# Attention, a gated block and four experts on one core: sums of h's tiles by accumulating transfers, signs in the gating, rest units on 64x64 quarters, and another list of work

## The chip, the core and the metric

One program on 1 core of a Trainium2 chip. The metric is the device time of the whole program in microseconds. TensorE (PE; PEld is its weight load), VectorE (DVE), ScalarE (ACT), GpSimd (POOL) and SyncE (SP, which issues the transfers) each run an instruction list of their own and wait for each other by semaphores.

## The reference

Three parts stand one behind the other, all in float32 (4 batches of 576 tokens, 8 heads of 64):

```python
kv = einsum('bhsd,bhse->bhde', k, v)
out = einsum('bhsd,bhde->bhse', q, kv)
x = out / sqrt(mean(out * out, -1) + 1e-6) * g_norm      # -> (2304, 512)

a, b = x @ w1, x @ w2                                     # 512 -> 1024
x = ((a * b) @ w3) @ w_out                                # -> (2304, 512)

p = probs / (probs.sum(-1) + 1e-9)                        # 4 experts
y = sum(p[:, e] * (maximum(x @ ew1[e], 0) @ ew2[e]) for e in range(4))
```

## The kernel before

Every large product is made of three TensorE passes on fp32r halves: high times high, low times high, high times low (lines 349, 350 and 351, function `mm3`). An operand is split into a high and a low tile by `split` (a cast, line 394, and a subtraction, line 399). Tiles are 128 partitions by 512 elements, 256 KB.

The work of the front part is written as a list of names, `FRONT`, and each name is a function that adds operations with an engine, a cost and the tiles it reads and writes. A planner (`Plan.order`) walks them in time: an engine takes the ready operation that stands earliest in the list, within a window, if tiles and PSUM banks are free. The result is a fixed order per engine; SP and GpSimd are engines of this plan like the others. The experts' part follows in a loop over three groups of tokens.

The parts that matter here:

- `unit b p` is attention for a batch and a pair of heads: loads of q, k and v, the product of keys and values (`outer_by_head`, line 803, 64x64 instructions, two heads in turn; `outer`, line 819), transposes of q (line 770), the product with q (line 847), and the norm (`normed_turned`; its root runs on GpSimd, lines 684 and 685). The last 64 tokens of each batch don't fill a tile; `rest_unit g` takes those of two batches for all heads. It writes the transposed q into two zeroed tiles `qr`, one for each batch, and line 883 makes 8 products of 128x128, two adding up in a place. An fp32 instruction of TensorE shows as two records.
- `bilinear_pair` and `bilinear_plain` make h = a * b from x, w1 and w2, by a scheme of seven products of sums in place of eight (Strassen's, in Winograd's form), and keep some tiles of h in DRAM (`ab0kept`, `ab1kept`).
- `row` and `turn` make w3 @ w_out once, `w3o`, with the sums of its blocks in `w3o_summed`.
- `mixed_product g n` multiplies h by w3o, seven products for each of two pairs of batches (`PAIR_PRODUCTS`): a11 b11, a12 b21, s2 t2, s1 t1, s3 t3, s4 b22, a22 -t4. Here t1 = b12 - b11, t2 = b22 - t1, t3 = b22 - b12 and -t4 = b21 - t2 are sums of h's tiles: 32 subtractions on VectorE (line 1240), each then split. Each product is four steps of six full-width products; its result is copied out of PSUM (`copied`) or added (`plus`, line 1274).
- After the front, expert weights are loaded (`e1raw`, `e2raw`, line 371), split, combined and stored to DRAM (`we`, `w2kept`; lines 384 and 1539), and loaded again for each group (line 1797 for w).

## Time and profile before

| | before |
|---|---|
| time, median of 3 runs | 1094.87 us (1094.67 to 1096.27) |
| the profiled execution | 1096.5 us |
| its span | 1094.7 us |
| TensorE busy | 1085.6 us, 99% |
| VectorE busy | 862.2 us, 79% |
| ScalarE busy | 634.2 us, 58% |
| GpSimd busy | 47.7 us, 4%, 61 instructions |
| moved by DMA | 286.5 MB, mean 262 GB/s |

The page is read by stage, since its shares are means over stages with different limits. Attention and the products for h lie between 0 and about 246 us, w3 @ w_out until 284, the products of h with it until 372, and the experts behind. A matmul's length in a timeline overlaps the next one's; the pace is the distance between starts.

### The profile page before, as it was taken

To read this page: it belongs to the slowest core of one execution; us is meant where nothing else is said; L and a number is where in the kernel's file an instruction comes from. 1 tells how busy PE (TensorE), PEld (TensorE's weight loads), DVE (VectorE), ACT (ScalarE), POOL (GpSimd) and SP (SyncE) were. 2 spreads that over 40 slices of the span, in tenths; PEclk is the share of its full clock that TensorE was granted. 3 is DMA by queue.
4 is the path that set the end of the run, shared out by engine and by line. 5 is a ranking of instruction groups with operands and counts; after the bars stand their busy time and mean duration, and the time that the engine had idled before them with its cause. 6 is when DMAs were issued, how large, how long until landed. Compare 5 with 4: busy or idle time off the path is not lost.

```text
span 1094.7 us, 18502 instructions
## 1 busy us (share of the span) xinstructions
PE 1085.6 (99%) x6411; PEld 987.4 (90%) x6411; DVE 862.2 (79%) x1692; ACT 634.2 (58%) x1369; POOL 47.7 (4%) x61
## 2 busy tenths in 40 slices
PE   8999999999999999999999999999999999999998
PEld 7888888888888999999899999999999999999998
DVE  4888989889988887888788874567688866485896
ACT  6888647888765655844564565534455555443531
POOL 6513000000000000000000000000000000000000
PEclk9999999999999999999999999999999999999999
DMA  9989798864500799989999997777779867676756
GB/s 325 307 265 334 273 345 271 250 160 89 174 1 7 263 356 349 333 302 295 364 350 328 342 347 250 273 250 256 251 262 353 296 232 246 233 278 223 274 163 196
DMA packets 177538, 286.50 MB, mean 262 GB/s; under 512 B 36388, under 2 KB 85028, under 8 KB 177444
## 3 DMA queue, kind: packets, MB, share of 16 engines
q1 hardware_dynamic: 177120, 285.05, 77.8%
q8 instruction: 51, 0.84, 0.3%
q14 instruction: 43, 0.35, 0.1%
q10 hardware_dynamic: 324, 0.26, 0.1%
HBM read 198.22 MB, written 82.84 MB: 257 GB/s over the span
## 4 chain that ended last, share of the span: by engine, by line
PE 93%; DMA 4%; DVE 1%; SPq 1%; ACT 1%; issue 0%; ACTq 0%; DVEq 0%
PE b L350 24%; PE b L349 24%; PE b L351 24%; PE b L1821 19%; PE b L770 1%; PE b L847 1%; DMA e1raw<-in_moe_w_dram 1%; DMA kv<-in_v_dram 1%; DMA w<-w2kept 1%; DMA w1raw<-in_moe_w_dram 1%; DMA kv<-in_k_dram 1%; PE b L803 1%; PE b L819 0%; SPq L371 0%; DMA e2raw<-in_moe_w_dram 0%
## 5 line engine op out<-in xcount | busy, mean ns | idle before, releaser
L1821 PE MATMUL b<-w,hth 128*128 128x512 f32 x588 | 208.4, 394 | 0.1
L758 ACT COPY u<-b 128x384 f32<-128x384 f32 (+1 forms) x183 | 91.9, 502 | 196.2 <-PE b L351 194.5
L1657 DVE TENSOR_TENSOR u<-u,b 128x384 f32<-128x384 f32 x144 | 79.4, 552 | 110.0 <-PE b L351 52.0
L1821 PE MATMUL b<-w,htl 128*128 128x256 f32 x588 | 156.0, 279 | 0.0
L1821 PEld LDWEIGHTS b<-w,hth 128*128 128x128 f32 x588 | 108.9, 188 | 19.6 <-DVE acc L1849 0.5
L1821 PEld LDWEIGHTS b<-w,htl 128*128 128x128 f32 x588 | 110.7, 188 | 3.0
L1849 DVE SCALAR_TENSOR_TENSOR acc<-b,pn,acc 128x512 f32<-128x512 f32 x123 | 85.5, 745 | 29.8 <-PE b L1821 29.5
L394 ACT CAST hth<-s 128x384 fp32r<-128x384 f32 x144 | 69.7, 512 | 44.0 <-DVE s L1757 43.3
L1668 ACT ACTIVATE u<-u 128x384 f32<-128x384 f32 x108 | 56.9, 527 | 47.0 <-DVE u L1657 46.8
L399 DVE TENSOR_TENSOR htl<-s,hth 128x384 fp32r<-128x384 f32 x144 | 75.5, 550 | 6.2 <-ACT hth L394 6.1
L399 DVE TENSOR_TENSOR htl<-u,hth 128x384 fp32r<-128x384 f32 x108 | 55.9, 550 | 2.2 <-ACT hth L394 2.2
L351 PE MATMUL b<-wdh,htl 128*128 128x512 f32 x144 | 56.7, 393 | 0.0
L350 PE MATMUL b<-wdl,hth 128*128 128x512 f32 x144 | 56.6, 393 | 0.0
L349 PE MATMUL b<-wdh,hth 128*128 128x512 f32 x144 | 56.0, 389 | 0.0
L394 ACT CAST hth<-u 128x384 fp32r<-128x384 f32 x107 | 51.2, 510 | 0.3
L349 PE MATMUL b<-w,hth 128*128 128x256 f32 x168 | 47.6, 283 | 0.7 <-DMA w<-w2kept 0.7
L350 PE MATMUL b<-w,hth 128*128 128x256 f32 x168 | 47.5, 283 | 0.0
L351 PE MATMUL b<-w,htl 128*128 128x256 f32 x168 | 47.5, 283 | 0.0
L349 PE MATMUL b<-th,weh 128*128 128x512 f32 x112 | 44.1, 394 | 0.0
L350 PE MATMUL b<-tl,weh 128*128 128x512 f32 x112 | 43.7, 390 | 0.0
L351 PE MATMUL b<-th,wel 128*128 128x512 f32 x112 | 43.6, 389 | 0.0
L1757 DVE TENSOR_TENSOR s<-u 128x384 f32<-128x384 f32 x72 | 37.5, 550 | 3.4 <-ACT u L1668 3.4
(310 smaller groups left out, 3150.8 us busy)
## 6 DMA issues: line engine op xcount, KB each, us to landing
w<-w2kept SPq DMA_DIRECT2D x126, 512.0 KB, 4.9
we<-we SPq DMA_DIRECT2D x240, 256.0 KB, 5.0
we<-weh SPq DMA_DIRECT2D x48, 256.0 KB, 3.5
we<-wel SPq DMA_DIRECT2D x48, 256.0 KB, 3.6
e2raw<-in_moe_w_dram SPq DMA_DIRECT2D x20, 512.0 KB, 5.5
w3raw<-in_moe_w_dram SPq DMA_DIRECT2D x16, 512.0 KB, 4.6
e1raw<-in_moe_w_dram SPq DMA_DIRECT2D x16, 512.0 KB, 4.8
w2kept<-wth SPq DMA_DIRECT2D x32, 256.0 KB, 3.9
```

Of the source, the lines that this page charges most:

```text
L349: nc.tensor.matmul(ps, w[0], x[0], start=first, stop=False, skip_group_check=more)
L350: nc.tensor.matmul(ps, w[0], x[1], start=False, stop=False, skip_group_check=more)
L351: nc.tensor.matmul(ps, w[1], x[0], start=False, stop=last, skip_group_check=more)
L394: nc.scalar.copy(to(dst.high.tile), value(src.tile))
L399: nc.vector.tensor_tensor(out=to(dst.low.tile), in0=value(src.tile), in1=to(dst.high.tile), op=ALU.subtract)
L758: lambda e: nc.scalar.copy(to(dst.tile), value(src.tile)) if e == "act"
L770: nc.tensor.transpose(ps[:, c], raw[:, c], ident)
L1657: lambda _: nc.vector.tensor_tensor(out=t[:, :W], in0=base[:, :W], in1=ps[:, :W], op=ALU.add),
L1668: lambda eng: nc.scalar.activation(out=t[:, :W], in_=src[:, :W], func=ACTF.Relu)
L1757: lambda eng: nc.vector.tensor_tensor(out=t[:, :W], in0=x[:, :W], in1=y[:, :W], op=op),
L1821: nc.tensor.matmul(ps.tile if whole_width else ps[:, 0:256], (h.high if whole_width else h.low)[:, c], both if whole_width else raw[:, r, ...
L1849: nc.vector.scalar_tensor_tensor(out=a.tile, in0=ps.tile, scalar=sc, in1=a.tile, op0=ALU.mult, op1=ALU.add)
```

## The change

- The 32 subtractions for t1 to t4 go from VectorE to the DMA: SP copies a tile (`copy_of`), and GpSimd issues a transfer that adds another tile to it (`added`, with `accum_op=ALU.add`). For t1, b12 is added to in place where it lies in the core's memory. That is 32 accumulating transfers and 16 more copies of 256 KB.
- A transfer can add and not subtract, so some of h's tiles get a minus sign: `negative` says which, and `times_signed` puts it into the multiplication that makes the tile. The seven products, their order and the signs of their results follow: `s1 t1` comes first, and results leave PSUM negated (`turned_round`) or by subtraction (`less`).
- The sums of blocks of weights are made in their own tile: two operations of 256 columns and one of 512 in place of four of 256 (`block_weights`, `w3o_summed`).
- A rest unit copies the transposed q once, whole (`qt`), and makes 16 products of 64x64, each on one of four quarters of TensorE, in place of 8 of 128x128; `qr` and its zeroing go; its norm reads two banks.
- `FRONT` is another list, in which units, rest units, weights and rows of w3 stand in other places.

TensorE's instructions are otherwise the same in number and form. The diff, cut to its core (of `FRONT` the first line):

```diff
-THREE_BANKS = ((0, 3), (1, 3))
+THREE_BANKS = ()
-EARLY = (0, 1, 2, 3, 4, 5, 6, 7, 8, 9, 12, 16)
+EARLY = (0, 1, 2, 3, 4, 5, 6, 7, 8, 9, 10, 12, 16)
+REST_INNER = 0.68
...
-    "norm_scale, weight 1 4, unit 0 0, unit 1 0, unit 1 1, weight 1 0, unit 1 3, unit 1 2, unit 0 1, unit "
+    "norm_scale, weight 1 4, unit 0 0, unit 1 0, unit 1 3, weight 1 0, unit 1 1, unit 1 2, unit 0 1, unit "
...
-        qs = []
-        while len(rest_q) < 2:
-            rest_q.append(zeroed("qr"))
-        for i in range(2):
-            s = rest_q[i]
-
-            def cut(t, c=slice(i * REM, (i + 1) * REM)):
-                return t.rearrange("p (h c) -> p h c", h=HP)[:, :, c]
-
-            evacuate(s, pq, 256, cut, cut)
-            qs.append(s)
-        po = bank()
+        qt = half("qt")
+        evacuate(qt, pq, 512, whole, whole)
+        po = [bank(), bank()]
 
         def inner(e):
-            for h in range(HP):
-                c = slice(h * P, (h + 1) * P)
-                for i in range(2):
-                    own, at = kvb[2 * g + i][h // 2], h % 2 * 2 * P
+            for p in range(HP):
+                for h, i in ((0, 0), (1, 1), (1, 0), (0, 1)):
+                    rows = slice(h * D, (h + 1) * D)
+                    own, at = kvb[2 * g + i][p // 2], p % 2 * 2 * P + h * (P + D)
                     nc.tensor.matmul(
-                        po[:, c], qs[i][:, c],
-                        own[:, at:at + 2 * P].rearrange("p (b c) -> p b c", c=D)[:, 0:4:3], start=i == 0, stop=i == 1,
+                        po[h][i * REM:(i + 1) * REM, p * D:(p + 1) * D],
+                        qt[rows, p * P + i * REM:p * P + (i + 1) * REM], own[rows, at:at + D],
+                        start=True, stop=True,
                     )
 
-        add({"pe": 1.72}, inner, reads=qs + kvb[2 * g] + kvb[2 * g + 1], writes=[po])
+        add({"pe": REST_INNER}, inner, reads=[qt] + kvb[2 * g] + kvb[2 * g + 1], writes=po)
...
+    def times_signed(t, x, sign):
+        if sign > 0:
+            nc.vector.tensor_tensor(out=t, in0=t, in1=x, op=ALU.mult)
+        else:
+            nc.vector.scalar_tensor_tensor(out=t, in0=x, scalar=sign, in1=t, op0=ALU.mult, op1=ALU.mult)
+
+    def negative(b, f):
+
+        return b < B and (b % 2 == 1) == (f < KF // 2)
...
-            lambda e: nc.vector.tensor_tensor(out=t[:, :n], in0=t[:, :n], in1=pb[:, :n], op=ALU.mult),
+            lambda e: times_signed(t[:, :n], pb[:, :n], sign),
...
+            s21 = half("s21")
+            left, right = (bufs[0], 0), (bufs[1], 1)
+
+            def sums(n, make, reads, writes):
+                add({"dve": t_dve(n)}, lambda _: nc.vector.tensor_tensor(**make()), reads=reads, writes=writes)
+
+            sums(256, lambda: dict(out=block(0, 0), in0=block(0, 1), in1=block(0, 0), op=ALU.subtract), [], [left])
+            sums(
+                512, lambda: dict(
+                    out=blocks(s21.tile), in0=block(1, 1).unsqueeze(2).to_broadcast([P, 2, 2, P]),
+                    in1=blocks(views[0](bufs[0].tile)), op=ALU.add,
+                ), [left, right], [s21],
+            )
+            sums(
+                256, lambda: dict(
+                    out=block(0, 1), in0=block(1, 0), in1=blocks(s21.tile)[:, :, 0], op=ALU.subtract,
+                ), [s21, right], [left],
+            )
+            split(pairs[2], s21, 512)
+            split(pairs[3], left, 512, whole, views[0])
...
     PAIR_PRODUCTS = [
-        ("a11", "b11", 0, True, "c11"), ("a12", "b21", 1, True, "c11"), ("s2", "t2", 0, False, "c12"),
-        ("s1", "t1", 1, True, None), ("s3", "t3", 0, False, "c22"), ("s4", "b22", 1, False, "c12"),
-        ("a22", "-t4", 0, False, "c21"),
+        ("s1", "t1", 1, True), ("a11", "b11", 0, True), ("s2", "t2", 0, False), ("a12", "b21", 1, False),
+        ("-s3", "t3", 0, False), ("s4", "b22", 1, False), ("a22", "t4", 0, False),
     ]
...
-                x, y = {
-                    "t1": ("b12", "b11"), "t2": ("b22", "t1"), "t3": ("b22", "b12"), "-t4": ("b21", "t2"),
-                }[name]
-                x, y, t = operand(x, i), operand(y, i), half(name)
-                add(
-                    {"dve": t_dve(512)},
-                    lambda e: nc.vector.tensor_tensor(
-                        out=t.tile, in0=x.tile, in1=y.tile, op=ALU.subtract
-                    ),
-                    reads=[x, y], writes=[t],
+                ab_sums[g, name, i] = {"t1": first_sum, "t2": second_sum, "t3": third_sum, "t4": last_sum}[name](
+                    {n: ab[at] for n, at in places.items()}, i
                 )
-                ab_sums[g, name, i] = t
             return ab_sums[g, name, i]
+
+        def copy_of(x):
+            t = half("ab")
+            load(t, (whole, x))
+            return t
+
+        def added(t, x):
+            add(
+                {"pool": 1.2}, lambda _: nc.gpsimd.dma_start(out=t.tile, in_=x[:, :], accum_op=ALU.add),
+                reads=[x], writes=[t], latency=3.2, hold=0.1,
+            )
+            return t
+
+        def first_sum(x, i):
+            ab_sums[g, "b12", i] = copy_of(x["b12"])
+            return added(x["b12"] if x["b12"].kind == "h" else copy_of(x["b12"]), x["b11"])
+
+        def second_sum(x, i):
+            return added(copy_of(x["b22"]), operand("t1", i))
+
+        def third_sum(x, i):
+            return added(ab_sums[g, "b12", i], x["b22"])
+
+        def last_sum(x, i):
+            return added(operand("b21", i), operand("t2", i))
...
+        def turned_round(to, ps):
+            add(
+                {"act": t_act(512, True) + 0.1, "dve": t_dve(512)},
+                lambda e: nc.scalar.activation(out=to.tile, in_=ps.tile, func=ACTF.Copy, scale=-1.0) if e == "act"
+                else nc.vector.tensor_scalar(out=to.tile, in0=ps.tile, scalar1=-1.0, scalar2=None, op0=ALU.mult),
+                reads=[] if to is ps else [ps], writes=[to], free=True,
+            )
+
+        def less(to, t, ps):
             add(
                 {"dve": t_dve(512)},
-                lambda _: nc.vector.tensor_tensor(out=t.tile, in0=t.tile, in1=ps.tile, op=ALU.add),
-                reads=[ps], writes=[t], free=True,
-            )
-
-        if target:
-            j0, b = (int(target[1]) - 1) * 2, (b0, b1)[int(target[2]) - 1]
-            for j, ps in enumerate(banks):
-                (plus if at else copied)(b, j0 + j, ps)
-                if target == "c22":
-                    plus(b, j0 + j, pair_banks[g][1][j])
-
-
-
+                lambda _: nc.vector.tensor_tensor(out=to.tile, in0=t.tile, in1=ps.tile, op=ALU.subtract),
+                reads=[ps] if to is t else [t, ps], writes=[to], free=True,
+            )
+
+        for j in range(2):
+            first, second = (pair_banks[g][at][j] for at in range(2))
+            c11, c12, c21, c22 = (b0, j), (b1, j), (b0, j + 2), (b1, j + 2)
+            made = {"s1": c22, "a12": c11, "s4": c12, "a22": c21}.get(left)
+            if made:
+                xf[made] = half("xf")
+            if left == "s1":
+                turned_round(xf[c22], second)
+            elif left == "a11":
+                turned_round(second, first)
+            elif left == "s2":
+                turned_round(first, first)
+            elif left == "a12":
+                turned_round(xf[c11], second)
+                less(second, xf[c22], first)
+            elif left == "-s3":
+                less(xf[c22], xf[c22], first)
+            elif left == "s4":
+                evacuate(xf[c12], second, 512, whole, whole)
+            elif left == "a22":
+                turned_round(xf[c21], first)
```

Three places of the order, before and after.

TensorE at the first rest unit, before (`x` turned by the identity, then the unit's products; `th`, `weh` and the like belong to h's products):

```order
L351 MATMUL b<-th,wel 128x512
L770 MATMUL b<-ident,x 128x128 x4
L883 MATMUL b<-kvb,qr 128x128 x8
L349 MATMUL b<-th,weh 128x512
L350 MATMUL b<-tl,weh 128x512
L351 MATMUL b<-th,wel 128x512
```

and after:

```order
L352 MATMUL b<-xth,wel 128x512
L779 MATMUL b<-ident,x 128x128 x4
L883 MATMUL b<-kvb,qt 64x64 x16
L350 MATMUL b<-th,weh 128x512
L351 MATMUL b<-tl,weh 128x512
L352 MATMUL b<-th,wel 128x512
```

Eight products of 128x128 became sixteen of 64x64; the step moved forward in the program.

GpSimd at its end, before (the roots of the norm, then the end):

```order
L684 TENSOR_SCALAR ss<-ss 128x8
L685 TENSOR_TENSOR ss<-ss,power 128x8
L684 TENSOR_SCALAR ss<-ss 128x8
L685 TENSOR_TENSOR ss<-ss,power 128x8
L2116 UNCONDITIONAL_BRANCH
L2116 ISA
```

and after (`u` and `ab` are tiles of h in the core's memory, `ab0kept` and `ab1kept` those in DRAM):

```order
L689 TENSOR_SCALAR ss<-ss 128x8
L690 TENSOR_TENSOR ss<-ss,power 128x8
L1271 DMA u<-u 128x512 x4
L1271 DMA ab<-ab0kept_928 128x512
L1271 DMA ab<-ab0kept_979 128x512
L1271 DMA ab<-ab0kept_2448 128x512
L1271 DMA ab<-ab0kept_2558 128x512
L1271 DMA ab<-u 128x512 x4
L1271 DMA ab<-ab 128x512 x4
L1271 DMA ab<-u 128x512 x4
L1271 DMA ab<-ab1kept_2305 128x512
L1271 DMA ab<-ab1kept_2315 128x512
```

All accumulating transfers stand behind the last root, in the order in which the sums are used.

SP at the end of the products with w3o, before (`ab` is h, `e1raw` and `e2raw` are expert weights as they come, `we` and `w2kept` their stored halves):

```order
L371 DMA ab<-ab1kept_2522 128x512
L371 DMA e1raw<-in_moe_w_dram 128x4x256
L371 DMA e2raw<-in_moe_w_dram 128x2x512
L384 DMA we_0_0_4453<-weh 128x512
L371 DMA e1raw<-in_moe_w_dram 128x4x256
L371 DMA e2raw<-in_moe_w_dram 128x2x512
L384 DMA we_0_1_4505<-wel 128x512
L384 DMA we_0_2_4509<-we 128x512
```

and after:

```order
L372 DMA ab<-ab1kept_1724 128x512
L372 DMA e1raw<-in_moe_w_dram 128x4x256
L372 DMA e2raw<-in_moe_w_dram 128x2x512
L372 DMA e1raw<-in_moe_w_dram 128x4x256
L372 DMA e2raw<-in_moe_w_dram 128x2x512
L372 DMA e1raw<-in_moe_w_dram 128x4x256
L385 DMA we_0_0_4515<-weh 128x512
L1597 DMA w2kept_0_0_4526<-wdh 128x256
L1597 DMA w2kept_1_0_4536<-wdh 256x1x256
L385 DMA we_1_0_4587<-weh 128x512
```

Three more expert loads stand ahead of the first store of a split weight. SP at the last unit's loads, before:

```order
L371 DMA q<-in_q_dram 64x8x64 x2
L384 DMA ab1kept_1171<-ab 128x512
L371 DMA q<-in_q_dram 128x2x256
L384 DMA w_3_0_1_1197<-wel 128x512
L371 DMA kv<-in_k_dram 128x2x256
L384 DMA w_3_1_0_1215<-weh 128x512
L371 DMA kv<-in_v_dram 128x2x256
```

and after:

```order
L372 DMA q<-in_q_dram 64x8x64 x2
L385 DMA ab1kept_1160<-ab 128x512
L372 DMA q<-in_q_dram 128x2x256
L372 DMA kv<-in_k_dram 128x2x256
L372 DMA kv<-in_v_dram 128x2x256
L385 DMA w_3_0_1_1205<-wel 128x512
L385 DMA w_3_1_0_1218<-weh 128x512
```

The unit's keys and values now follow its queries at once, ahead of the stores of w.

## Rows read from the trace of the kernel before

**Rows 1.** The page: busy time of each engine, granted clock by slice, the chain by engine.

```profile
PE 1085.6 (99%) x6411; PEld 987.4 (90%) x6411; DVE 862.2 (79%) x1692; ACT 634.2 (58%) x1369; POOL 47.7 (4%) x61
...
PEclk9999999999999999999999999999999999999999
...
PE 93%; DMA 4%; DVE 1%; SPq 1%; ACT 1%; issue 0%; ACTq 0%; DVEq 0%
```

**Rows 2.** Waits of TensorE: engine, line, releaser, us in total, times, longest.

```profile
PE b L803 <- DMA kv<-in_v_dram: 1.6, 2, 1.3
...
PE b L349 <- DMA w<-w2kept: 0.7, 1, 0.7
PE b L770 <- DMA q<-in_q_dram: 0.5, 2, 0.3
PE b L350 <- DVE xrl L736: 0.4, 1, 0.4
```

**Rows 3.** Windows: length; PE, PEld, DVE, ACT, POOL busy (count); PEclk; DMA share; GB/s.

```profile
0.00:27.00 27.00, 23.48 (x352) 21.45 (x353) 13.18 (x22) 17.78 (x47) 16.19 (x29) 1.00 0.96 326
301.00:328.00 27.00, 27.00 (x121) 22.37 (x120) 24.10 (x41) 16.09 (x30) 0.00 (x0) 1.00 0.00 1
328.00:356.00 28.00, 28.00 (x136) 23.64 (x136) 24.88 (x46) 14.44 (x33) 0.00 (x0) 1.00 0.03 10
383.00:410.00 27.00, 27.00 (x137) 24.38 (x136) 23.41 (x47) 14.19 (x29) 0.00 (x0) 1.00 1.03 356
410.00:438.00 28.00, 28.00 (x143) 25.57 (x143) 21.87 (x43) 15.21 (x32) 0.00 (x0) 1.00 1.02 349
465.00:493.00 28.00, 27.29 (x211) 27.12 (x210) 23.15 (x51) 13.48 (x30) 0.00 (x0) 1.00 0.89 302
```

**Rows 4.** Timeline of TensorE at one rest unit: start, length, line, operation, count.

```profile
92.30 1.95 PE L883 MATMUL b<-kvb,qr 128*128 128x128 f32 x16
94.01 0.48 PE L349 MATMUL b<-th,weh 128*128 128x512 f32 x1
```

**Rows 5.** Timeline of TensorE at two products of keys and values.

```profile
29.65 1.26 PE L803 MATMUL b<-kv 64*64 64x64 f32 x36
30.84 0.66 PE L770 MATMUL b<-ident,q 128*128 128x128 f32 x4
...
96.95 0.69 PE L819 MATMUL b<-kv 128*64 128x64 f32 x16
```

**Rows 6.** Timeline of SP (its queue's issues) around the end of w3's products.

```profile
284.47 0.50 SPq L371 DMA_DIRECT2D e2raw<-in_moe_w_dram  x1
354.40 0.34 SPq L384 DMA_DIRECT2D we<-weh  x1
```

**Rows 7.** Timeline of TensorE at the wait for w.

```profile
477.95 0.28 PE L351 MATMUL b<-w,htl 128*128 128x256 f32 x1
478.94 0.36 PE L349 MATMUL b<-w,hth 128*128 128x256 f32 x1 [0.71 <-DMA w<-w2kept]
```

**Rows 8.** Timeline of SP before that wait.

```profile
471.03 2.15 SPq L1797 DMA_DIRECT2D w<-w2kept  x3
```

**Rows 9.** Timeline of SP at the last unit's loads.

```profile
67.95 0.33 SPq L384 DMA_DIRECT2D ab1kept<-ab  x1
...
70.71 0.43 SPq L371 DMA_DIRECT2D kv<-in_k_dram  x1
```

**Rows 10.** DMA issues: tile, queue, count, size of one, median us to landing.

```profile
kv<-in_k_dram SPq DMA_DIRECT2D x8, 256.0 KB, 6.7
...
ab<-ab0kept SPq DMA_DIRECT2D x8, 256.0 KB, 3.4
...
q<-in_q_dram SPq DMA_DIRECT2D x4, 128.0 KB, 3.7
```

**Rows 11.** GpSimd by line: its slowest operation (line, shapes, count, busy, mean ns, idle).

```profile
L685 POOL TENSOR_TENSOR ss<-ss,power 128x8 f32<-128x8 f32 x18 | 31.3, 1737 | 1.5
```

**Rows 12.** VectorE by line: one of the six groups of h's sums, 32 in all.

```profile
L1240 DVE TENSOR_TENSOR t<-u 128x512 f32<-128x512 f32 x8 | 5.4, 685 | 0.0
```

127 lines of the change are left out of this document (63 added, 64 removed), and 26 rows, old and new, of the table FRONT.

## Prediction

> **What bounds the kernel now.** I read the page first: TensorE is busy for 1085.6 of the 1094.7 us, the chain that ended last is 93% TensorE, and the granted clock reads 9 tenths or more in every slice, the upper of its two levels [rows 1]. Then the waits of TensorE: six lines, none over 1.6 us; beyond the start-up they name the second weights (0.7 us), the queries (0.5) and one operand of a product (0.4) [rows 2]. Then the stages, by windows: where w3's products run, 301 to 356 us, TensorE is busy for all of 27 and all of 28 us, VectorE for 24.1 of 27, and the DMA engines rest (share 0.00 and 0.03); from 383 us on the DMA engines are full (1.03) and TensorE still has 27.00 of 27; only 465 to 493 shows 27.29 of 28 [rows 3]. The reader is to see two things. A busy VectorE (89%) is no bound while TensorE never waits for it. And what can be won is what TensorE itself executes, or a wait of the few in rows 2. The change takes 22 us off VectorE, but off the path.
>
> **The change part by part.**
>
> *Rest units, on the path.* Before, one rest unit's inner product holds TensorE from 92.30 to 94.01 us: 1.71 us for 8 instructions, shown as 16 records [rows 4]. There are two units, so 3.42 us in all. After, each is 16 instructions on 64x64 quarters, 32 records, 64 in both. The nearest row is the keys-times-values product, whose 64x64 instructions alternate between two quarters: 36 records from 29.65 to 30.84 us, 33 ns each, the change of form included [rows 5]. With two in flight, as there, the new form costs 64 x 33 ns = 2.1 us and saves 1.3. The new order names four different quarters in turn; if four run together, the pace halves to 17 ns, 1.1 us, and with about 0.3 us for changing the form around each unit (an estimate: what the 1.19 us of rows 5 leave over a pure two-quarter pace of about 26 ns) 1.6 to 1.7, which saves 1.8; without any cost of the change of form it would save 2.3. A reason excludes a loss here: fewer cells are multiplied, and no operand is larger. I take -1.9, near the four-quarter end, because the order was given all four quarters and the two-quarter row already shows that different quarters overlap.
> The Trainium skill, page "TensorEngine Tiling (Array Packing)", counts four independent 64x64 tiles in its Overview and says under Key Properties that changing the tiling mode drains the engine. No run here shows four at once; by it the saving would lie near 1.9.
>
> *Sums of h, off the path if they land in time.* Removed: 32 VectorE subtractions of 128x512, 0.68 us each [rows 12], 22 us. Added: 32 accumulating transfers of 256 KB issued by GpSimd, and 16 more SP copies of 256 KB ahead of them. Gain on the path: nothing, since TensorE loses no time in that stage [rows 3]. Cost: nothing if each sum lands before the split that reads it. GpSimd is free there (0.00 us busy [rows 3]); the 12 MB of copies and sums fall into 55 us in which the DMA engines rest, and at the 349 to 356 GB/s of rows 3 take 34 us. A copy of this size lands 3.4 us after its issue [rows 10]. In the new order the first sums stand 7 us of TensorE's work (five steps of six full-width products at 27.00/121 = 0.223 us each, 1.34 us a step) ahead of the step that needs them, the later ones 8 us and more. The first sixteen are used within twenty steps, 27 us. So GpSimd must hand out one sum in (27 + 7 - 3.4)/16 = 1.9 us. No row shows a transfer issued by GpSimd. The bounds come from SP's issue of the same size (0.33 us, rows 9) and from the slowest thing GpSimd does here, a power at 1.74 us [rows 11]: both under 1.9. I take zero; behind it, the whole pace over 1.9 us is lost sixteen times (first rival).
>
> *Signs, block sums in place, VectorE.* The signs ride in multiplications that stand there already; the block sums are one 512 and two 256 operations for four of 256; four additions less for xf. All lie on VectorE and ScalarE within 0.1 us of what they replace, beside a TensorE that does not wait. Zero. Negated results in PSUM hold a bank for one 0.7 us operation longer, at the end of a product of 24 x 0.223 = 5.4 us; the other bank pair is then in work. Zero.
>
> *SP around the end of the products.* Before, SP issues two expert loads, the second at 284.47 us, then stands at a store of a split weight until 354.40 [rows 6]; the DMA engines idle, and the saturated stretch follows. In it the load of w that TensorE waits for is issued at 471.03 [rows 8], and the product that needs it starts at 478.94 instead of about 478.07 [rows 7]: 0.87 us. After, five expert loads stand ahead of that store, so three loads of 512 KB (1.5 MB, 4.3 us at 350 GB/s) leave the saturated stretch. That covers 0.87 us. But the new order has three stores of its own ahead of one such load of w. Bounds 0 and -0.9; I take -0.7, nearer to the full gain, because the relief is several times the wait.
>
> *Loads of the last unit.* Before, its keys are issued at 70.71 us [rows 9] and multiplied at 96.95 [rows 5]. The new list brings that product 78 full-width products and one rest unit forward, some 22 us, to about 75 us. Its loads stand right behind a store of h that went out at 67.95 before [rows 9]; issued at 68.4 to 69.3 and landing 6.7 us later [rows 10], they arrive at 75.1 to 76.0. A wait of 0 to 1 us; the second rest unit's queries, also behind two stores, another 0 to 1 (3.7 us to land [rows 10], needed near 79.5). This is the added wait to look for: queued behind it on TensorE is everything. I take +0.3, because a wait of SP for a store's source moves with the same TensorE work as the consumer does. The front start stays as it was: the first 28 rows of TensorE and the first 24 of SP do not differ, so the 3.5 us of TensorE's gaps in the first 27 us stay [rows 3].
>
> **Sum.** -1.9 + 0 + 0 - 0.7 + 0.3 = -2.3 us. The profiled execution took 1096.5 us (span 1094.7), 1.6 above the median; 1096.5 - 2.3 = 1094.2, and on the median 1094.87 the same step gives 1092.6.
>
> **The rivals.**
> 1. *GpSimd's sums come too slowly* (ends slower). Place: the products with an accumulated operand, between about 288 and 365 us. It decides from 1.9 us per sum: at 2.3 us sixteen sums are 16 x 0.4 = 6.4 us late, and the later ones, which have more room, add nothing. Then 1092.6 + 6.4 = 1099.0. A lighter form, 2.1 us, gives 3.2 us and 1095.8. For it: no row shows this path, SP's later copies wait for these sums, and the expert loads stand behind those copies, so a late sum delays SP too. Against it: nothing else runs on GpSimd, and the DMA engines are idle. The Trainium skill, page "DMA: Bandwidth & Descriptors", section "Anatomy of one DMA — SWDGE (gpsimd) path", fits 2.0 us plus bytes over 436 GB/s, 2.6 us for 256 KB (an estimate), as the duration of one; read as a pace without overlap, 16 x 0.7 = 11 us would be lost and the time be 1104. Its page "SBUF — State Buffer", section "SBUF: two separate sides", adds that GpSimd cannot write descriptors while VectorE runs certain two-port copies; no row here shows either.
> 2. *No change that can be measured.* The rest units save only the two-quarter 1.3 us, the load of w is late again behind the new stores (0), and the last unit's loads cost 0.5: -0.8, 1094.1. For it: both small terms rest on distances of under 1 us in queues. It includes the case that the sums bring nothing at all, which the rows say anyway.
> 3. *The last unit's loads are late by 2 us* and the rest is as forecast: -0.6, 1094.3. For it: before had over 20 us to spare there and after has none.
>
> **How the numbers follow.** A measurement of this kernel can tell about 0.2% from no change, 2.2 us: under 1092.7 is faster, over 1097.1 slower. Forecast 0.62. Its own range is 1090.6 to 1093.8: the rest units run from -2.3 to -1.3, the load of w from -0.9 to 0, and a few of the waits left in rows 2 may go too; it reaches further down from 1092.6 than up, so I give 0.40 of it to faster and 0.22 to the same. Rivals 2 and 3 together 0.17, all the same. Rival 1 0.21: 0.17 slower, 0.04 the lighter form, which is the same. Faster 0.40, same 0.43, slower 0.17. The range goes from 1090.6, the forecast's good end, to 1097.3, just past the bound of slower, which leaves out most of rival 1.
>
> **What would show it.** Right: two stretches of about 0.8 us in place of 1.71 at the rest units; TensorE busy for the whole of every window from 290 to 365 us, with accumulating transfers on GpSimd's queue and a VectorE freed by about 22 us; expert loads issued before SP's long stand; no wait for w's load near 478 us. Wrong: a line of TensorE (or of ScalarE and VectorE, at a split) waiting for a transfer from GpSimd; a wait for keys or queries near 75 to 80 us; 64x64 records 33 ns apart. If the time falls by 5 us or more, something was on the path that rows 2 and 3 do not show, and the reading above is wrong.

## The result, and the profile after

The changed kernel takes 1112.79 us, median of 4 runs (1110.63 to 1114.3), beside 1095.57 us for the kernel before on the same chip: a ratio of 1.015 [1.0135, 1.0166]. The forecast was 1092.6 us with a range up to 1097.3, so the change is slower by 17 us where a gain of 2 was forecast. The profiled execution took 1110.63 us; its span is 1108.9 us, 14.2 more than that of before.

The page of the changed kernel: busy times, granted clock by slice, and the queue that GpSimd fills.

```profile
PE 1087.6 (98%) x6443; PEld 986.5 (89%) x6443; DVE 843.4 (76%) x1649; ACT 633.5 (57%) x1354; POOL 76.5 (7%) x91
...
PEclk9999999999998999999999999999999999999999
...
q0 software_dynamic: 4608, 8.39, 4.3%
```

Against [rows 1] TensorE's busy time hardly moves (1085.6 to 1087.6 us), VectorE's falls by 18.8 us, and one slice of the clock falls to 8 tenths. So TensorE does not have more to do; it stands somewhere. The waits of TensorE say where:

```profile
PE b L351 <- DVE abl L402: 10.3, 1, 10.3
PE warm L449 <- POOL ident masks.py:199: 1.3, 1, 1.3
PE b L350 <- ACT b L767: 1.2, 1, 1.2
PE b L350 <- DVE b L1320: 1.1, 2, 0.7
PE b L350 <- DMA w<-w2kept: 0.9, 1, 0.9
PE b L856 <- ACT qt L767: 0.9, 1, 0.9
PE b L812 <- DMA kv<-in_v_dram: 0.8, 1, 0.8
```

One wait of 10.3 us stands at the head, on VectorE's half of a split (`abl`, line 402) in w3's products, where [rows 2] had nothing. Its place, in the timeline of TensorE:

```profile
324.46 0.39 PE L350 MATMUL b<-abh,w3oh 128*128 128x512 f32 x1
335.18 0.79 PE L351 MATMUL b<-abl,w3oh 128*128 128x512 f32 x1 [10.33 <-DVE abl L402]
335.77 0.63 PE L352 MATMUL b<-abh,w3ol 128*128 128x512 f32 x1
336.20 0.63 PE L350 MATMUL b<-abh,w3oh 128*128 128x512 f32 x1
```

To see how much of the 14 us this is, I added up, stretch by stretch, how far the starts of TensorE's matmuls stand apart beyond the steady pace of their shape (0.227 us at 512 columns, and so on): the time that TensorE loses, in us.

| stretch | before | after | sums on VectorE | plain copies |
|---|---|---|---|---|
| 0 to 30 | 5.1 | 4.2 | 4.4 | 4.4 |
| 30 to 140 | 6.8 | 6.8 | 7.1 | 7.8 |
| 140 to 280 | 0 | 0 | 0 | 0 |
| 280 to 380 | 0.5 | 14.9 | 1.6 | 0.0 |
| 380 to 520 | 0.9 | 1.5 | 1.9 | 1.2 |
| 520 on | 0.9 | 0.8 | 0.4 | 0.9 |

(The last two columns are experiments, below. Of the 6.8 us of before in the second row, 2.3 are the rest units' wide instructions themselves.) From before to after the differences add up to 14.0 us, and the row from 280 to 380 us, the stage of the sums, has 14.4.

What happens there is read backwards from that wait. Windows of the changed kernel (length; busy time of PE, PEld, DVE, ACT and POOL; PEclk; DMA share; GB/s):

```profile
265.00:345.00 80.00, 69.67 (x296) 57.06 (x295) 47.11 (x83) 44.87 (x80) 28.65 (x32) 0.91 0.99 244
325.00:330.00 5.00, 0.00 (x0) 0.00 (x0) 0.00 (x0) 0.00 (x0) 1.43 (x2) 0.72 1.09 263
330.00:335.00 5.00, 0.00 (x0) 0.00 (x0) 1.17 (x2) 0.00 (x0) 0.32 (x1) 0.50 0.94 230
335.00:340.00 5.00, 4.82 (x11) 3.80 (x12) 5.00 (x11) 3.59 (x8) 3.24 (x4) 0.50 0.57 97
340.00:345.00 5.00, 5.00 (x21) 4.05 (x20) 3.70 (x7) 1.63 (x4) 2.19 (x3) 0.91 1.07 178
```

From 325 to 330 us no engine computes, and the DMA engines are full (1.09). Where [rows 3] had a share of 0.00 and 0.03 and TensorE at work throughout, the whole stage now runs at 0.99. TensorE's clock falls to 0.50, its lower level, while TensorE stands, and stays there until after 340 us: 14 matmuls run 0.427 us apart instead of 0.227, another 2.8 us. The timeline of VectorE, and one row of ScalarE:

```profile
314.83 1.02 DVE L402 TENSOR_TENSOR abl<-ab,abh 128x256 fp32r<-128x256 f32 x2
333.83 2.50 DVE L402 TENSOR_TENSOR abl<-ab,abh 128x512 fp32r<-128x512 f32 x4 [17.98 <-DMA ab<-ab]
```

```profile
336.41 0.62 ACT L397 CAST abh<-ab 128x512 fp32r<-128x512 f32 x1 [13.33 <-DVE abl L402]
```

VectorE stands for 18 us ahead of one split, and ScalarE behind it. The operand of that split had landed at 313.7 us. What was missing was room: its low half is written into the tile (the same address in the program) that held t2, and the 25th sum, t4 = ... + t2, was still to read t2. GpSimd issued that sum at 327.32 us; its last packet landed at 333.74, and VectorE went on at 333.83. An accumulating transfer does not only deliver late, it also gives its source back late.

Why it was issued so late, in the timeline of GpSimd (three pieces of 32 sums; line 1271 is `added`):

```profile
279.78 0.88 POOL L1271 DMA_DIRECT2D ab<-ab0kept  x1 [2.21 <-PE b L352]
...
312.04 0.90 POOL L1271 DMA_DIRECT2D ab<-u  x1 [2.89 <-issue]
...
327.32 0.87 POOL L1271 DMA_DIRECT2D ab<-ab  x1 [3.69 <-issue]
329.44 0.87 POOL L1271 DMA_DIRECT2D ab<-ab  x1 [1.25 <-issue]
```

Handing out one sum takes GpSimd 0.88 us. But it often stands ahead of one although nothing in the profile holds it ("issue"), and then it starts 0.3 us after the third sum before it has landed: at 312.04 after 311.74, at 315.36 after 315.05, at 327.32 after 327.01, at 339.56 after 339.25. Three sums are in flight and no more. Each takes 3.4 to 10.2 us from issue to landing, so the 32 went out 2.3 us apart on average (270.03 to 342.49 us).

The queues between 265 and 345 us (packets, MB, share of 16 engines over the stretch):

```profile
q0 software_dynamic: 4495, 8.19, 57.7%
q1 hardware_dynamic: 7792, 11.27, 41.6%
```

57.7% of 80 us over 8.19 MB is 5.6 us of all 16 engines for a MB that is added. The plain transfers of the other queue take 33.3 us for 11.27 MB, 2.95 us per MB. Together the two fill the stretch.

### The profile page after: what moved, and what is told of

It is laid out like the page before. It is cut to its first block, busy times and chain, and to the rows that moved or that the text cites. A ratio compares the mean times of both kernels' runs of the same rounds, so it can differ in the third digit from the quotient of the medians.

```text
span 1108.9 us, 18566 instructions
## 1 busy us (share of the span) xinstructions
PE 1087.6 (98%) x6443; PEld 986.5 (89%) x6443; DVE 843.4 (76%) x1649; ACT 633.5 (57%) x1354; POOL 76.5 (7%) x91
## 4 chain that ended last, share of the span: by engine, by line
PE 92%; DMA 4%; issue 1%; DVE 1%; ACT 1%; POOL 1%; SPq 0%; POOLq 0%; ACTq 0%
PE b L350 24%; PE b L352 24%; PE b L351 23%; PE b L1879 18%; PE b L779 1%; PE b L856 1%; DMA e1raw<-in_moe_w_dram 1%; DMA w<-w2kept 1%; DMA kv<-in_v_dram 1%; PE b L812 1%; DMA w<-wel 1%; PE b L828 0%; DMA ab<-ab 0%; DMA w2raw<-in_moe_w_dram 0%; DMA u<-ab 0%
## 5 line engine op out<-in xcount | busy, mean ns | idle before, releaser
L767 ACT COPY u<-b 128x384 f32<-128x384 f32 (+1 forms) x179 | 89.6, 501 | 183.9 <-PE b L352 179.9
L402 DVE TENSOR_TENSOR abl<-ab,abh 128x512 fp32r<-128x512 f32 (+1 forms) x44 | 26.6, 640 | 36.3 <-DMA ab<-ab 18.0
```

The costliest lines, as they stand in the source:

```text
L402: nc.vector.tensor_tensor(out=to(dst.low.tile), in0=value(src.tile), in1=to(dst.high.tile), op=ALU.subtract)
L767: lambda e: nc.scalar.copy(to(dst.tile), value(src.tile)) if e == "act"
```

## The experiments

Ratios are against the kernel before in the same session, whose medians lay between 1095.07 and 1096.17 us. Diffs are against the changed kernel unless said otherwise; "lost" is the measure of the table above. My theory after the result: the accumulating transfers cost nearly all of it, by filling the DMA engines and by holding t2. Rivals: another part of the change; GpSimd's limit of three; the order that the planner made from too low a cost.

### Are the sums the cause, and is it the adding?

**Sums on VectorE**, everything else as changed:

```diff
...
-                {"pool": 1.2}, lambda _: nc.gpsimd.dma_start(out=t.tile, in_=x[:, :], accum_op=ALU.add),
-                reads=[x], writes=[t], latency=3.2, hold=0.1,
+                {"dve": t_dve(512)},
+                lambda _: nc.vector.tensor_tensor(out=t.tile, in0=x.tile, in1=y.tile, op=ALU.add),
+                reads=[x, y], writes=[t],
...
```

> The changed kernel with its 32 sums of h's tiles on VectorE again (additions of signed tiles into tiles of their own, without copies on SP for them and without any transfer on GpSimd); signs, list, rest units and block sums stay as changed, and the planner orders anew. Theory (all of the loss is the accumulating transfers: TensorE's 10.5 us wait at 325 us, 2.8 us at half clock behind it and 1.4 us of waits for results held back by the last sums): these 14.9 us go and the time lies within 1.5 us of before, 1094 to 1097, with no TensorE wait over 0.6 us between 280 and 400 us. Rival (the new list, the negated results or VectorE's load cost it): still over 1104, with a TensorE wait in that stretch named by VectorE.

1099.69 us (7 runs), 1.0039 [1.0027, 1.0051]. 13 of the 17 us are the sums. The stretch from 280 to 380 us loses 1.6 us instead of 14.9. Some 4 us over before remain, 2.7 above the expected range; the last group of experiments takes them up.

**Plain copies**, the same order of work and the same queue, without the additions:

```diff
-                {"pool": 1.2}, lambda _: nc.gpsimd.dma_start(out=t.tile, in_=x[:, :], accum_op=ALU.add),
+                {"pool": 1.2}, lambda _: nc.gpsimd.dma_start(out=t.tile, in_=x[:, :]),
```

> The changed kernel in the same order of work, with the 32 sums' transfers made plain copies on the same GpSimd queue (the additions are left out, so the sums are not computed). Theory, adding inside a transfer is what fills the DMA engines: GpSimd's queue occupies the engines about half as long for the same bytes (2.8 to 3.2 us of all 16 per 8.2 MB where the adding ones took 5.6 us per MB), transfers land within 3.5 to 5 us, the wait of TensorE on the low half at 325 us falls from 10.3 us to under 4 us, and the kernel takes 1099 to 1104 us. Rival, GpSimd's queue itself sets the pace (three transfers in flight, its descriptors): landing still takes 5 to 8 us, the wait stays at 8 us or more, 1109 to 1114 us.

1098.22 us (9 runs), 1.0026 [1.0016, 1.0035]. The theory holds, more fully than expected: the long wait is gone altogether, and the stretch loses 0.0 us. (The expectation's 2.8 to 3.2 us are meant per MB.) The queues between 265 and 345 us:

```profile
q1 hardware_dynamic: 8447, 11.43, 44.0%
q0 software_dynamic: 2560, 8.39, 28.5%
```

The same bytes on the same queue take 28.5% of 80 us, 2.7 us per MB, in 80 packets a transfer instead of 144. GpSimd hands one out in 0.55 us and does not stop at three:

```profile
299.63 2.20 POOL L1271 DMA_DIRECT2D ab<-u  x4
```

It stops at seven: the next one starts at 303.20 us, 0.3 us after the seventh before it has landed. So this run takes away the add and the limit of three; the next one tells the two apart. The shortest copies land after 2.2 to 2.4 us, where the shortest sum takes 3.4. So the queue of GpSimd is not slow; a transfer that adds takes twice the engines' time, 5.6 against 2.7 us per MB. The Trainium skill, page "Collectives: The Full Stack", section "The bandwidth ceiling: the fold count and why AG ≠ RS ≠ AR", says of the reductions that cores do among themselves that the add needs two source reads, two descriptors for a piece, and so half the rate. The trace here agrees with the factor, at 2.07 times the time and 1.8 times the packets; that the second read is the reason, no run here shows.

### Three in flight, or full engines?

**Twice the descriptor space** for GpSimd's queue. It takes room from one tile, so the second kernel is its control, with one tile less alone.

```diff
-TILES = 99
+TILES = 98
...
-    nc = _bacc.Bacc("TRN2", target_bir_lowering=False, num_devices=1, dynamic_dma_scratch_size=1024)
+    nc = _bacc.Bacc("TRN2", target_bir_lowering=False, num_devices=1, dynamic_dma_scratch_size=2048)
```

> The changed kernel with 2048 in place of 1024 bytes for GpSimd's descriptors, paid for by one tile less (98 for 99). In the changed kernel GpSimd issues sum n 0.3 us after sum n-3 has landed wherever nothing else holds it, so three are in flight at most. Theory A (the room for descriptors sets the pace): six or seven in flight, GpSimd issues as soon as its operands are there, the wait at 325 us shrinks to under 3 us, 1096 to 1101. Theory B (the DMA engines are full, 1.07 to 1.11 busy from 284 to 330 us): more in flight only land later each, 9 us or more from issue to landing, and the wait stays over 7 us, 1106 to 1114.

> The same with 98 tiles and the old 1024 bytes, to tell the tile from the room for descriptors. Both theories: like the changed kernel, a TensorE wait of 8 us or more near 325 us and 1108 to 1115; if it is better than that by over 5 us, the tile (another plan) and not the room explains the run beside it.

1115.23 us (4 runs), 1.017 [1.0151, 1.019], and the control 1119.68 us (2 runs), 1.0217 [1.0192, 1.0243]. The limit of three does come from the descriptor space: with twice of it seven sums are in flight, and the next goes out 0.3 us after the seventh before it has landed (310.10 after 309.83 us, 311.36 after 311.10). It buys 4.4 us and no more, and the sums then share the engines: they land 1.27 us apart while nothing else loads (345.88 to 353.53 us, seven sums), some 2.0 us apart beside other loads, and take up to 14 us each. TensorE's waits on splits, of the control and with twice the space:

```profile
PE b L351 <- DVE abl L402: 11.4, 4, 9.0
```

```profile
PE b L351 <- DVE abl L402: 3.1, 2, 2.9
```

The longest is 2.9 us instead of 9.0, but a wait for `w3osh`, which the control has too, grows from 3.5 to 5.9 us. Both times lie above every expected range: a plan with one tile less costs some 7 us by itself. Full engines set the pace; the limit of three only adds to it.

### Why does VectorE stand?

**Half of the sums back on VectorE** (t1 and t2), t3 and t4 by transfer:

```diff
...
         def second_sum(x, i):
-            return added(copy_of(x["b22"]), operand("t1", i))
+            return added_here(operand("b22", i), operand("t1", i))
...
```

> The changed kernel with the first half of the sums (t1 and t2) on VectorE and only the sixteen of t3 and t4 as accumulating transfers. Theory (each sum costs the DMA engines 1.3 us alone and about 2 us beside other transfers, and 32 of them with their copies are more than the stretch holds): half of them fit, TensorE waits under 2 us between 280 and 400 us, the clock stays at the upper level, 1097 to 1101. Rival (it is the late ones whose buffer VectorE writes again, however few there are): a wait of 5 us or more, named by VectorE, stays, 1104 to 1112.

1110.97 us (3 runs), 1.0136 [1.0119, 1.0153]. Half of the transfers, and nearly all of the loss. VectorE again stands ahead of a split until a transfer lands that reads the tile it wants:

```profile
340.32 0.69 DVE L402 TENSOR_TENSOR abl<-u,abh 128x512 fp32r<-128x512 f32 x1 [8.01 <-DMA ab<-ab]
```

That sum landed at 340.30 us. This is the rival: with half of the sums, one hand-over of a tile still costs nearly as much.

**An honest cost in the planner** (GpSimd 2.2 us for a sum, 7 us to land):

```diff
-                {"pool": 1.2}, lambda _: nc.gpsimd.dma_start(out=t.tile, in_=x[:, :], accum_op=ALU.add),
-                reads=[x], writes=[t], latency=3.2, hold=0.1,
+                {"pool": 2.2}, lambda _: nc.gpsimd.dma_start(out=t.tile, in_=x[:, :], accum_op=ALU.add),
+                reads=[x], writes=[t], latency=7.0, hold=0.1,
```

> The changed kernel with the planner told what a sum took: 2.2 us of GpSimd for 1.2, and 7.0 us to landing for 3.2; nothing else is edited, the order follows. Theory (the loss is an order made for transfers twice as fast: a split's buffer is taken from a sum that has not landed): the order no longer puts VectorE behind such a sum, the longest wait falls under 4 us, and what is left is work that the stretch lacks, 1098 to 1107. Rival (the DMA engines can't carry it in any order): waits of 10 us and more in all stay, 1109 to 1118.

1115.08 us (3 runs), 1.0176 [1.0159, 1.0193]. With these costs and the same list, VectorE again starts when a sum lands (335.95 after 335.76 us), TensorE waits 9.3 us there, and 2.8 more in a new place. This, too, is the rival's range. A better order may exist; better costs alone did not find it.

**The expert loads behind the sums**, in the same order of instructions otherwise: a write by GpSimd into the first load's tile, behind its last sum, holds SP.

```diff
...
+            def late(_):
+                nc.gpsimd.memset(raw1[:, 0, 0:8], 0.0)
+                nc.sync.dma_start(out=raw1[:, :, :], in_=src)
...
```

> The changed kernel, same order on every engine, but the first expert load waits for a small write of GpSimd that stands behind the last of its sums, so that no expert load is issued before all sums are. Theory (transfers compete: with the five expert loads in flight the sums landed 1.9 us apart, alone they land 1.3 to 1.5 us apart): the sum that VectorE waits for lands near 328 instead of 333.7 us, TensorE's wait falls from 10.3 to 4 to 6 us, 1103 to 1108. Rival (the room for three transfers and the wait for buffers set it alone): the wait stays within 1.5 us of 10.3 and the time within 2 us of 1112.8, or later, by loads that now come late.

1109.25 us (3 runs), 1.0122 [1.0105, 1.0139]. The 25th sum lands at 330.77 instead of 333.74 us, VectorE goes on at 330.86, and TensorE's wait there is halved to 5.0 us, as expected; the time stays 1 us above the expected range, and waits for results behind it are longer (2.6 us, 1.1 in the changed kernel). So the five expert loads, which the change moved into this stage, are half of the long wait and some 3 us of the time. (A wait of 1.5 us for a weight at 139 us stands ahead of all sums and of these loads.)

**t2 in tiles of its own** that no split is given (8 tiles, so 91 remain for the others), and the same with the expert loads late:

```diff
-TILES = 99
+TILES = 91
...
-            return added(copy_of(x["b22"]), operand("t1", i))
+            return added(copy_of(x["b22"], True), operand("t1", i))
```

> The changed kernel in which the eight tiles of t2, which the last sums read, lie in eight tiles of their own that nothing else is written into (91 tiles for the rest in place of 99, order anew). In the changed kernel the buffer of such a tile was handed to the low half of another split while the sum that reads it had not landed: VectorE stood there from 315.9 to 333.8 us, and the sum landed at 333.7. Theory (that hand-over turns a late sum into a stand of VectorE, and with it of TensorE): the sums land as late as before, up to 331 us and more, but VectorE goes on, TensorE's wait there falls under 3 us and the clock stays up; with the waits of the front 1098 to 1104. Rival (the sums are too late for their own readers anyway): TensorE waits 6 us or more in all between 280 and 380 us, 1106 or more.

> Both at once: tiles of their own for t2, and the expert loads behind the last sum. Theory (two separate causes, the hand-over and the loads that compete): no wait over 1.5 us between 300 and 380 us, 1096 to 1102, at most as long as with own tiles alone. Rival (loads that come later cost as much behind): the waits move to the experts' first products near 390 to 500 us, 1102 or more.

1112.13 us (3 runs), 1.0148 [1.0121, 1.0175], and 1111.86 us (3 runs), 1.0152 [1.0124, 1.0181]. In time nothing is won, as the rival said. The trace shows the mechanism all the same: from 280 to 365 us VectorE stands nowhere longer than 4.4 us, and 280 to 380 us lose 4.6 us instead of 14.9, although the sums are as slow as before. But the eight tiles are missing elsewhere (one tile less alone cost some 7 us in the control above). These are the windows of the first of the two (columns as above):

```profile
250.00:280.00 30.00, 26.14 (x104) 20.15 (x103) 26.83 (x53) 28.10 (x38) 0.00 (x0) 0.89 0.61 136
280.00:380.00 100.00, 97.43 (x439) 80.44 (x439) 70.42 (x137) 62.52 (x124) 28.54 (x32) 0.98 0.81 199
```

TensorE now loses 9.4 us from 250 to 280 us, waits for operands (3.9 us for `w3th`) and a lower clock (0.89), where the changed kernel had 30.00 of 30 at 1.00. The late loads change nothing here; why, no run shows. What the hand-over alone costs in time stays open too, since every run without it has something else changed.

### What are the last four microseconds?

**The quarters alone**, in the kernel before, planned at their new cost and at the old one:

```diff
+REST_INNER = 0.68
...
-        add({"pe": 1.72}, inner, reads=qs + kvb[2 * g] + kvb[2 * g + 1], writes=[po])
+        add({"pe": REST_INNER}, inner, reads=[qt] + kvb[2 * g] + kvb[2 * g + 1], writes=po)
```

> The kernel before with nothing but the rest units on 64x64 quarters (and their norm over two banks). Theory: the inner product takes 0.63 us in place of 1.71, two units save 2.1 us, 1093.4 or a ratio of 0.998. Rival: the planner's order moves and the saving goes into another wait: a ratio within 0.0007 of 1, with the two stretches just as short.

> The kernel before with the rest units on 64x64 quarters, as in the run of the rest units alone, but with the planner's old cost of 1.72 us for their products, so that the plan's times stay as they were. Theory (the rest units do save 2.1 us, and what the other run lost, 4 us of waits at 108 to 115 us and 1 to 2 us of loads at 470 us, came from an order that moved): 1092.5 to 1094.5. Rival (the two banks, or ScalarE's whole copy of q, make the waits themselves): the waits near 110 us stay, 1098 to 1101.

1100.12 us (4 runs), 1.004 [1.0025, 1.0055], and 1100.13 us (7 runs), 1.0038 [1.0026, 1.005]. The part of the change that I was surest of makes the kernel slower when it is put in alone, although the two units take 2.2 us less. With the old cost:

```profile
104.40 0.39 PE L352 MATMUL b<-xth,wel 128*128 128x512 f32 x1
106.48 0.63 PE L778 MATMUL b<-ident,x 128*128 128x128 f32 x4 [1.69 <-DVE x L693]
```

The last unit's product starts at 98.78 us, and by 104.63 TensorE has nothing left before it needs that unit's turned x; the norm's chain (ScalarE, VectorE, GpSimd, VectorE) takes until 106.48. In the kernel before, the product starts at 100.00 and x is turned at 107.25: TensorE had 7.25 us to do in between, now it has 5.85. Most of the difference is the second rest unit, which stands there (101.33 us before, 99.77 now) and is 1.1 us shorter: it was part of the chain's cover. And the chain was longer, by a step on GpSimd, the addition of a constant under the root (line 684 before, 688 here), in the timelines of GpSimd of before and of this kernel:

```profile
102.50 0.24 POOL L684 TENSOR_SCALAR ss<-ss 128x8 f32<-128x8 f32 x1 [4.00 <-DVE ss L678]
```

```profile
101.64 2.22 POOL L688 TENSOR_SCALAR ss<-ss 128x8 f32<-128x8 f32 x1 [6.93 <-DVE ss L682]
```

It ends 0.1 us behind a row of VectorE operations that runs without a gap from 100.48 to 103.75 us, as if held by it.

**That addition left out**, in three kernels (the one with quarters alone, before, and the changed one with the sums on VectorE):

```diff
-            nc.gpsimd.tensor_scalar(out=flat, in0=flat, scalar1=1e-6 * D, scalar2=None, op0=ALU.add)
             nc.gpsimd.tensor_tensor(out=flat, in0=flat, in1=power, op=ALU.pow)
```

> The kernel before with the rest units on quarters (planned at the old cost, 1100.1 us), and GpSimd's addition of a small constant under the norm's root left out, so that the root is one GpSimd instruction and not two; order as it was. In that kernel the addition (128x8) took 2.22 us at 101.64 us, beside an unbroken row of VectorE operations, instead of 0.24, and TensorE then waited 1.69 us for a turned x. Theory, any GpSimd instruction that has to begin there is held until VectorE's row ends: the root takes the hold over (about 3.7 us in place of 1.67), the wait for x stays over 1.2 us, 1099 to 1100.5 us. Rival, the hold belongs to the addition: the root stays at 1.7 to 2.2 us, the wait goes, 1097.5 to 1098.5 us.

> The control: the kernel before with the same addition left out, same order. Both theories: 1094 to 1096 us, ratio 0.999 to 1.001, since its chains were covered. A ratio under 0.998 would say that GpSimd's step is on the path in the kernel before too.

> The changed kernel with the 32 sums on VectorE (1099.7 us) and the same addition left out, same order. If GpSimd's step is a large part of the 4 us over before (it takes up to 0.9 us instead of 0.24 in this kernel), 1097 to 1098 us; if the 4 us are waits behind ScalarE and VectorE, as its waits for copies and splits say, 1099 to 1100 us.

1100.46 us (5 runs), 1.004 [1.0027, 1.0052]; 1095.97 us (11 runs), 1.0002 [0.9993, 1.001]; 1100.81 us (5 runs), 1.0047 [1.0033, 1.0061]. At that place the rival is right: two roots in a row, the first beside the same row of VectorE's operations, take 3.57 us together, and the wait of 1.69 us for x is gone (its turning starts at 104.45 us without a stop). (Not everywhere: at 91.17 us a root takes 2.99 us in place of 1.64, and one in the kernel before without the addition takes 3.23 at 104.80 us.) In time nothing comes of it. Other waits take its place:

```profile
PE b L350 <- ACT u L765: 2.2, 3, 1.5
PE b L350 <- ACT xrh L736: 1.7, 1, 1.7
PE b L350 <- DVE b L1096: 1.5, 1, 1.5
```

So GpSimd's step is real and is not what the 4 us hang on. My theory of the lost cover explains one wait, not the time.

**Squares on ScalarE made wide**, on top of the sums on VectorE: in the changed kernel eight narrow squares (line 676) stand ahead of the copies that TensorE waits for at 76 and 81 us.

```diff
-EARLY = (0, 1, 2, 3, 4, 5, 6, 7, 8, 9, 10, 12, 16)
+EARLY = (0, 1, 2, 3, 4, 5, 6, 7, 8, 9, 10, 11, 12, 13, 16)
```

> The changed kernel with the 32 sums on VectorE (as in the run with the sums on VectorE, 1099.7 us), and the eight narrow squares with accumulators on ScalarE at 73.5 and 77.5 us made one wide square each plus a sum on VectorE, as the kernel before has them at other tiles. Theory, the two waits of TensorE at 76 and 81 us (1.04 and 1.36 us) come from these squares standing ahead of the copies of turned tiles in ScalarE's queue: they go, and the kernel takes about 1097 us, ratio 1.001 to 1.002, at best no more than before. Rival, the wait only changes its name (VectorE's sum and norm chain come last instead): 1099 to 1100 us, as without the edit.

1099.01 us (6 runs), 1.0034 [1.0022, 1.0046]: the rival. The wait at 76 us goes; the one at 81 us stays for the most part (0.9 us, now on a split by ScalarE), another of 0.6 us appears at 107.87 us, the first values come 0.8 us later, and w3's products lose 0.9 us more.

**The old rest units, the old list, and both**, each on top of the sums on VectorE. The last of them is the kernel before with the signs (and the order of the seven products that goes with them) and the block sums in place alone. Of the list the first line:

```diff
-    "norm_scale, weight 1 4, unit 0 0, unit 1 0, unit 1 3, weight 1 0, unit 1 1, unit 1 2, unit 0 1, unit "
+    "norm_scale, weight 1 4, unit 0 0, unit 1 0, unit 1 1, weight 1 0, unit 1 3, unit 1 2, unit 0 1, unit "
```

> The changed kernel with the 32 sums on VectorE (1099.7 us, 1.004 of before) and the rest units as before (8 products of 128x128); signs, block sums and the new list stay. Theory, the 4 us left over come from the rest units' quarters, whose two short products no longer cover the norm chain beside them: these go, 1095.5 to 1097 us, ratio up to 1.0013. Rival, the new list: 1099 to 1101 us, ratio 1.0035 or more, the two waits at 76 and 81 us stay.

> The changed kernel with the 32 sums on VectorE and the list of before (with its settings); quarters, signs and block sums stay. Theory, the rest units' quarters: 1099 to 1101 us, a wait for a turned x of 1 to 2 us near 106 us as in the kernel before with quarters alone. Rival, the new list: 1094 to 1096.5 us, the saving of 2.2 us shows in part.

> The kernel before with the signs and the block sums in place alone (sums on VectorE, rest units and list as before). Theory, these two edits are free, as predicted: 1095 to 1096.5 us, ratio 0.999 to 1.001. Rival, one of them is part of the 4 us: 1097 us or more.

1098.9 us (9 runs), 1.003 [1.002, 1.0039]; 1098.15 us (11 runs), 1.003 [1.0021, 1.0039]; 1098.37 us (9 runs), 1.003 [1.0018, 1.0042]. With the 1.0039 of both new, the four corners can't be told apart. So neither the list nor the quarters is the remainder: signs and block sums alone already cost 0.3%, where the forecast had zero, the quarters alone cost 0.4%, and together they cost no more than either. The waits of TensorE in the kernel with signs and block sums alone:

```profile
PE b L820 <- DMA kv<-in_v_dram: 2.2, 2, 1.9
PE warm L449 <- POOL ident masks.py:199: 1.3, 1, 1.3
PE b L787 <- DVE x L701: 1.0, 1, 1.0
PE b L787 <- DMA q<-in_q_dram: 1.0, 1, 1.0
PE b L350 <- ACT u L775: 0.6, 1, 0.6
```

Its span is 3.6 us over that of before, and the first 140 us lose 3.3 of them: first keys and values later (2.2 us of waits against the 1.6 of [rows 2]), a turned x, queries. In the other three corners there are also two to four waits of 1 to 2 us, but elsewhere: 115.71 us with the old list, 77.52 and 289.17 us with the old rest units. Every edit changes what the planner sees and with it the order of everything behind. That the order of before, with no wait over 1.3 us, is a lucky one, and that most others cost some 3 us in waits between TensorE, ScalarE and VectorE, fits all these kernels. But no run shows it as the cause; several orders of one and the same work would. Nor is it the order alone: the changed kernel, the plain copies and the late loads have one and the same order of instructions up to the sums, and their traces show a wait of 0, 1.1 and 1.5 us for the same weight at 138 to 139 us. It also stays open why the medians of some kernels (4.6 us over before with the sums on VectorE) lie further up than their profiled executions (1.4 us): the single executions of that kernel spread over 4 us, those of before over 3 in the same session.

No kernel here was faster than the one before.

## Why the prediction was wrong, step by step

**What bounds the kernel: right.** TensorE was, and what the change took off VectorE (18.8 us of busy time) gave nothing.

**Rest units, -1.9: right in size.** The rows that answer to [rows 4], the 32 records and the next start:

```profile
86.12 0.69 PE L883 MATMUL b<-kvb,qt 64*64 64x64 f32 x32
86.75 0.50 PE L350 MATMUL b<-th,weh 128*128 128x512 f32 x1
...
93.34 0.69 PE L883 MATMUL b<-kvb,qt 64*64 64x64 f32 x32
93.96 0.33 PE L779 MATMUL b<-ident,x 128*128 128x128 f32 x1
```

0.63 and 0.62 us for a unit instead of 1.71: -2.2 us, close to the end of four quarters without a cost of changing form (-2.3). The pure two-quarter pace of 26 ns, from which the prediction took 0.3 us for changing the form, stands in no run: inside the product of [rows 5] the records lie 29 ns apart and inside the new one 15 ns, which leaves some 0.14 us at the ends of either. What the step left out is that a product can be the cover of another unit's chain. It asked what hides an edit's cost, and not what the removed time had been hiding: the quarters alone made the kernel 4 us slower, and the lost cover explains one wait of 1.7 us of that.

**Sums of h, 0: the step that failed.** I bounded the pace of the sums by what it takes to *hand one out* (0.33 to 1.74 us, [rows 9, 11]). That was sound in itself: it took 0.88. But the pace was set by landing, with three in flight, and landing by the DMA engines. The engines I had put down with 12 MB (12.6 as the page counts) at 349 to 356 GB/s, 34 of 55 us, as if a MB that is added cost what a MB that is copied costs. At the measured 5.6 us per MB the 8.4 MB of sums alone are 47 us, and with some 4 MB of copies at 2.95, 12 us more: 59 us for 55. The first estimate of the engines' time, done at twice the price for an add, would have turned the forecast. No row of before showed that price, and I had no upper bound for it: the bounds stood on the issue alone.

**Rival 1** named the right place and half of the mechanism, and its threshold (1.9 us a sum; 2.3 measured) was passed. Its price was wrong: 6.4 us spread over the first sixteen sums, and nothing later. The first sixteen cost TensorE nothing; the loss is one wait at the 25th, whose source was promised to a split on VectorE, and then the clock: 10.3 + 2.8 + 1.1 us for results late behind it. I had followed who waits for what a transfer writes, and not who waits for what it reads.

**SP around the end of the products, -0.7: wrong.** The loads moved ahead of the long stand as forecast (five expert loads from 313.92 to 319.92 us; the store behind them at 375.89), but w came 0.9 us late all the same, at 492.28 us. And the gain had a price that I did not see: these loads ran among the sums, and cost about half of the long wait (5.3 of 10.3 us) and some 3 us of the time.

**Loads of the last unit, +0.3: wrong reason.** The keys came in time: they landed at 72.84 us and the values at 74.17, for a product that started at 74.61, although 78 products and a rest unit are 19 us by the prediction's own figures and not 22. What TensorE waits for at 76.27 and 80.88 us (0.85 and 1.20 us) are copies by ScalarE, which stand behind sixteen short instructions for narrow squares, 73.47 to 75.1 and 77.53 to 79.2 us:

```profile
73.47 0.23 ACT L676 ACTIVATE x<-b 128x64 f32<-128x64 f32 x1 [0.35 <-PE b L856]
73.59 0.19 ACT L676 ACTIVATION_READ_ACCUMULATOR x<-b 128x1 f32 x1
```

I had followed the queue of SP, which the new list moves, and not that of ScalarE, in which the same list puts a product's squares ahead of the next unit's copies. By the table above, the first 140 us lose in waits some 1.4 of the 2.3 us that the quarters give.

**Signs and block sums, 0:** in the run with these alone 3 us were lost. Each operation costs what I said (a signed multiplication 0.69 us, as the plain one; block sums of 0.69 and 0.42 us); what the whole then costs, the sum of the operations did not tell.

## What to carry to other kernels

Before work goes from an engine to the DMA, add up the DMA engines' time in that stretch at the price of that kind of transfer: one that adds counts twice its bytes, and the loads moved there by the same change count too. Then follow both ends of each transfer: who waits for what it writes, and who waits to reuse what it reads, up to an in-order engine that stands for both. And when a piece of work on the bounding engine gets shorter, ask which chain ran under its cover; with a planned order, try such an edit alone before it is counted as a gain.

## What the runs showed of the hardware

- GpSimd's addition on 128x8 took 0.24 us as a rule and 2.22 us (3.22 in the run with the old rest units) beside an unbroken row of VectorE operations; in the kernel before it took 0.24 us at 102.50 us beside such a row, too. With the addition left out, a root took 2.99 us instead of 1.64 at one place (3.23 in the kernel before), and was hardly held at another. The Trainium skill, page "SBUF — State Buffer", section "SBUF: two separate sides", tells of a port that the two share and that one holds at a time. The long steps fit that; why some steps got through, the runs don't show.
- An accumulating transfer of 256 KB takes about twice the DMA engines' time of a plain one: 5.6 against 2.7 us of 16 engines per MB on the same queue, 144 packets against 80. At its quickest it lands 3.4 us after its issue (2.2 for the plain one), and 1.27 us apart is the closest that several in a row landed.
- With 1024 bytes of descriptor space three such transfers are in flight, and the fourth's issue stands on GpSimd; with 2048 bytes it was seven, and seven plain ones with 1024. The issue itself takes 0.88 us (0.55 for a plain one).
- Sixteen fp32 products of 64x64 on four quarters take 0.63 us, 20 ns a record, where two quarters gave 33 ns [rows 5].
- A stand of TensorE of 10 us cost 2.8 us more: its granted clock fell to 0.50, the lower of its two levels (1.2 GHz), during it, and the first 14 matmuls behind it ran at that level.
